# Windowed attention and mixer: first tiles with per-head maxima, weights converted behind x, inner layer two tiles behind, keys loaded first

## The chip, the core and the metric

The kernel runs on one core of a Trainium2 chip. Five engines work side by side, each through its own queue in order: TensorE (PE), VectorE (DVE), ScalarE (ACT), GpSimd (POOL) and SyncE (SP), which here issues nearly all DMAs. They wait for one another by semaphores. Matrix products land in PSUM banks; everything else lies in SBUF. The metric is the device time of one execution in microseconds (us).

## The reference

Attention over a causal window of 64 positions, and a mixer (two small MLPs, one over tokens, one over channels) on its result:

```python
scores = scale * np.matmul(q, k.transpose(0, 1, 3, 2))     # q, k, v: 8 x 8 heads x 576 x 64
mask = (rel >= 0) & (rel < 64)
scores = np.where(mask, scores, -1000000000.0)
scores = scores - np.max(scores, axis=-1, keepdims=True)
attn = np.exp(scores)
attn = attn / (np.sum(attn, axis=-1, keepdims=True) + 1e-09)
x = np.matmul(attn, v)                                     # heads side by side: 8 x 576 x 512
h = np.maximum(xt @ w_tok1, 0.0) @ w_tok2                  # xt: x transposed; inner width 256
u = x + h.transpose(0, 2, 1)
h2 = np.maximum(u @ w_ch1, 0.0) @ w_ch2                    # inner width 1536
return u + h2
```

The weights arrive as 64-bit floats.

## The kernel before

The first third of the run is one loop over 36 attention tiles (lines 499 to 561). A tile is 128 queries, two blocks of 64, of all eight heads, with the two blocks of keys that the window reaches. Heads are handled in two halves (u = 0 and 1) of four. For a tile:

- qk (scores, s): TensorE, two PSUM banks.
- softmax: the maxima, on VectorE. For the tiles up to 6, TensorE has added the mask by a matmul (line 287), so VectorE takes one reduction over four heads (line 309) and scales the result (line 310). For later tiles one operation per head adds the mask, scales, writes to SBUF and gives the maximum (line 316).
- softmax_exp: eight exponentials on ScalarE with their sums (line 325).
- pt_transpose: TensorE transposes (pp), ScalarE copies to SBUF (pt, line 334).
- av: TensorE, the weighted sum of v (xp, line 344); recip and norm on VectorE (lines 352, 353, 358) give x.
- split_x: x as a high part (xhi, ScalarE) and the rest (xlo, GpSimd), since the mixer's products are done in two parts.
- tok1: the inner layer over tokens (h, line 389), six to ten matmuls a tile, collected over the tiles of a batch. Its result goes through hhi (ScalarE, line 400) and hlo (VectorE, line 409).
- tok2: pieces of the second token layer (up, lines 430 and 437), eight for each batch, which ScalarE copies out (line 442). They fill TensorE from tile 7 on.

Between these stand the conversions of the weights, 28 jobs. Each loads a slice (raw, line 236), VectorE makes 32-bit floats of it in six operations (front part lines 204 to 207, back part lines 216 to 219), GpSimd adds (w, line 221), ScalarE writes the high part and GpSimd or, for the second token weight, VectorE the low part (t1hi, t1lo, t2hi, t2lo, line 104).

The order is written by hand: the body of the loop is the order on each engine, and JOBS, PIECES, TOK1_FROM and TOK1_SLOW say at which step a conversion, a piece of tok2 or the inner layer of a tile comes. In step i the maxima and exponentials of tile i + 1, the weighted sum of tile i and the scores of tile i + 2 are issued. After the loop the channel layers follow (three plain chunks, then pairs of chunks by a scheme with seven products), nearly all TensorE.

Of the kernel before, what the change touches and what calls it, by code (L numbers as in the profile page):

```python
# [42 lines left out]
JOBS = {i: 1 if 0 <= i < 6 or i == 12 or i > 6 and i % TPP not in (0, 3, 5) else 0 for i in range(-1, 37)}  # L43
PIECES = {22: (1, 0), 23: (1, 0), 31: (1, 0), 32: (1, 0), 33: (1, 0), 34: (1, 0), 35: (3, 0), 36: (2, 1)}

TOK1_FROM, TOK1_SLOW, TOK2_FROM = 2, 4, 7

N_PE, N_EARLY = 7, 4
# [35 lines left out]
def mixer_kernel(ctx: ExitStack, tc: tile.TileContext, qh, kh, vh, wt1, wt2, wc1, wc2, out):  # L84
# [38 lines left out]
    with ExitStack() as actx:  # L123
# [26 lines left out]
        maskr = [pa.tile([P, P], F32R, name=f"maskr{m}") for m in range(2)]  # L150
        identr = pa.tile([P, P], F32R, name="identr")
# [6 lines left out]
        def warm(k):  # L158
            for _ in range(k):
                nc.tensor.matmul(idle, zero[:, :P], zero, start=True, stop=True)  # L160

        make_identity(nc, ident)
        nc.scalar.copy(identr, ident)
        for m in (1, 0):
            nc.gpsimd.memset(mask[m], 0.0)
            for half in range(2):
                mh = mask[m][half * BLK:(half + 1) * BLK]
                nc.gpsimd.affine_select(out=mh, in_=mh, compare_op=ALU.is_ge, fill=NEG,
                                        base=-1, pattern=[[1, P]], channel_multiplier=-1)
                nc.gpsimd.affine_select(out=mh, in_=mh, compare_op=ALU.is_ge, fill=NEG,  # L170
                                        base=BLK, pattern=[[-1, P]], channel_multiplier=1)
            if m == 1:
                nc.gpsimd.memset(mask[1][0:BLK, 0:BLK], NEG)
            nc.scalar.copy(maskr[m], mask[m])
# [94 lines left out]
        def qk(i):  # L269

            qt, on_pe = loaded[i][0], i < N_PE
            s = []
            for u in range(2):

                if i == 1:
                    tag, bufs = "h", 2
                elif (i, u) == (N_PE, 1) or 2 <= i < N_PE and (2 * i + u) % 3 == 0:
                    tag, bufs = "up", 1
                else:
                    tag, bufs = "s", 2  # L280
                s.append(ps.tile([P, 4, P], F32, name=f"s{i}_{u}", tag=tag, bufs=bufs))
                s_ps[i, u] = s[u]
                if i == 0 and u == 0:
                    warm(4)
                if on_pe:
                    mk = maskr[1 if tile_blocks(i)[0][1] == 0 else 0]
                    nc.tensor.matmul(s[u], identr, mk.unsqueeze(1).to_broadcast([P, 4, P]), start=True, stop=False,
                                     skip_group_check=True)
            if i == 0:
                warm(3)  # L290
            for j in range(4):
                for u in range(2):
                    r = slice(u * BLK, (u + 1) * BLK)
                    for half, (b, n) in enumerate(tile_blocks(i)):
                        so = s[u][half * BLK:(half + 1) * BLK, j].rearrange("p (n c) -> p n c", n=2)
                        nc.tensor.matmul(so, qt[r, j, half], kbs[b][r, n:n + 2, j],  # L296
                                         start=not on_pe, stop=True, skip_group_check=on_pe)

        def softmax(i, u):
# [7 lines left out]
            nmu = nm.rearrange("p (j u) -> p j u", u=2)[:, :, u]  # L307
            if i < N_PE:
                nc.vector.tensor_reduce(out=nmu, in_=s_ps[i, u], axis=AX.X, op=ALU.max, negate=True)
                nc.vector.tensor_scalar_mul(nmu, nmu, scale)  # L310
                return
# [7 lines left out]
        def softmax_exp(i, u):  # L319
            e = e_sb[i, u]  # L320
            nm, sm = st[i]
            src, by = (s_ps.pop((i, u)), scale) if i < N_PE else (e, -1.0)
            for h in range(4):
                g = 2 * h + u
                nc.scalar.activation(e[:, h], src[:, h], AF.Exp, bias=nm[:, g:g + 1], scale=by,  # L325
                                     accum_out=sm[:, g:g + 1])
# [152 lines left out]
        job_load()  # L479
# [6 lines left out]
        load_v(0)  # L486
        nc.sync.dma_start(kbs[0][:, 8:], kh[0, :, 8:])
# [9 lines left out]
        job_convert_a()  # L497
        job_convert_b()
        qk(0)
        for i in range(-1, NT + 1):  # L500
# [13 lines left out]
            early = i < N_EARLY  # L514
# [6 lines left out]
            if i == 0:  # L521
                softmax(1, 1)
            if early and i > 0:
                norm(*normed.pop())
            if 0 <= i < NT:
                ri = recip(i)
            if i not in (4, 5):
# [10 lines left out]
            if i >= N_PE - 1:  # L538
# [4 lines left out]
            if i + 1 < NT and i != 0:  # L543
                softmax(i + 1, 1)
            if i < N_PE - 1:
                for _ in range(n_jobs):
                    job_convert_a()
            if i < N_PE - 1:
# [5 lines left out]
            if N_PE - 1 <= i < NT - 1:  # L554
                softmax_exp(i + 1, 1)
            for _ in range(n_jobs):
                job_convert_b()
            if 0 <= i < NT:
                xp = av(i, pts)
                if i + 1 < N_EARLY:  # L560
                    normed = [(i, xp, ri)]
                else:
                    norm(i, xp, ri)
            finish_h_low()
            if i + 2 < NT:
# [411 lines left out]
```

## Time and profile before

| | us |
|---|---|
| median of 3 runs | 832.0 (831.72 to 832.02) |
| the profiled execution | 832.27 |
| its span, first to last instruction | 830.5 |
| TensorE busy in the span | 814.5 (98%) |
| VectorE busy | 508.6 (61%) |
| ScalarE busy | 336.4 (41%) |
| GpSimd busy | 104.8 (13%) |

Busy time is the time in which an engine has an instruction in work. The shares are means over the whole run: VectorE and ScalarE do most of their work in the first 250 us. Most of the 16 us in which TensorE has nothing in work lie in the first 60 us. The time outside the span, 1.77 us, is start and end of the execution.

### The profile page before, as it was taken

Reading aid. Unit: us, or ns where it says so; the run is one execution under the profiler, and the core shown is the slowest. Engines: PE = TensorE matmul, PEld = TensorE weight load, DVE = VectorE, ACT = ScalarE, POOL = GpSimd, SP = SyncE. Lnnn points to the kernel's source line nnn. Section 1 sums busy time; section 2 is a strip of 40 time slices with the busy share of each in tenths; the row PEclk is TensorE's granted clock in tenths of the full one; section 3 lists DMA queues with packets and bytes.
Section 4 is the critical chain, followed back from the end, with each engine's and each line's share of the span. In section 5 each row is a group of like instructions: output and inputs, shape, how many; then the busy total and the mean of one; then the engine's idle time right before and its main releaser. Section 6 shows DMA issues by size and latency. Waiting matters only on the chain.

```text
span 830.5 us, 15190 instructions
## 1 busy us (share of the span) xinstructions
PE 814.5 (98%) x5878; PEld 678.9 (82%) x5878; DVE 508.6 (61%) x1288; ACT 336.4 (41%) x1017; POOL 104.8 (13%) x110
## 2 busy tenths in 40 slices
PE   8879999999999999999999999999999999999998
PEld 6668888888888878888888888878888888888886
DVE  6888988788782993774444535267625277525252
ACT  6788888888874440331221202033202033202020
POOL 4434543444330000000000000000000000000000
PEclk9999999999999999999999999999999999999999
DMA  9667778587545528633505442324543334532002
GB/s 346 202 216 243 237 251 277 192 280 273 179 133 196 168 82 257 203 98 120 197 1 210 157 190 95 133 95 169 168 176 117 111 120 169 175 144 89 1 1 101
DMA packets 69671, 136.51 MB, mean 164 GB/s; under 512 B 7008, under 2 KB 39264, under 8 KB 67680
## 3 DMA queue, kind: packets, MB, share of 16 engines
q1 hardware_dynamic: 67488, 133.71, 47.4%
q10 hardware_dynamic: 2112, 1.84, 0.7%
q8 instruction: 46, 0.75, 0.4%
q14 instruction: 25, 0.20, 0.1%
HBM read 104.66 MB, written 30.87 MB: 163 GB/s over the span
## 4 chain that ended last, share of the span: by engine, by line
PE 83%; DVE 9%; ACT 4%; issue 2%; DMA 1%; POOLq 0%; POOL 0%; DVEq 0%; ACTq 0%; SPq 0%
PE gp L876 19%; PE op L664 11%; PE gp L656 8%; PE up L437 5%; PE h L389 5%; PE op_2a L664 4%; PE op_4a L664 4%; PE op_0a L664 4%; PE op_0b L664 4%; PE op_2b L664 4%; PE op_4b L664 4%; PE xp L344 3%; PE s L296 3%; PE pp L332 3%; PE up L430 2%; ACT e L325 2%
## 5 line engine op out<-in xcount | busy, mean ns | idle before, releaser
L876 PE MATMUL gp<-m,w1hi 128*128 128x512 f32 x504 | 155.5, 390 | 0.7 <-DVE x L884 0.7
L876 PEld LDWEIGHTS gp<-m,w1hi 128*128 128x128 f32 x504 | 94.5, 188 | 21.0 <-DVE x L884 1.5
L876 PE MATMUL gp<-m,w1lo 128*128 128x512 f32 x252 | 98.2, 390 | 0.0
L325 ACT ACTIVATE e<-e,nm 128x128 f32<-128x128 f32 x232 | 90.7, 401 | 0.1
L643 ACT ACTIVATE ghi<-x 128x512 fp32r<-128x512 f32 x54 | 34.1, 632 | 119.9 <-DVE x L886 68.3
L880 ACT COPY x<-gp 128x512 f32<-128x512 f32 x18 | 10.4, 578 | 143.2 <-PE gp L876 143.2
L644 DVE SCALAR_TENSOR_TENSOR glo<-x,ghi 128x512 fp32r<-128x512 f32 x54 | 37.4, 693 | 38.1 <-ACT ghi L643 38.1
L643 ACT ACTIVATE ghi<-gp 128x512 fp32r<-128x512 f32 x50 | 29.8, 597 | 70.0 <-PE gp L656 70.0
L656 PE MATMUL gp<-uhi,w1hi 128*128 128x512 f32 x144 | 56.1, 390 | 0.0
L656 PE MATMUL gp<-ulo,w1hi 128*128 128x512 f32 x144 | 56.1, 390 | 0.0
L656 PE MATMUL gp<-uhi,w1lo 128*128 128x512 f32 x144 | 56.1, 389 | 0.0
L316 DVE CUSTOM_DVE_ANT_0 e<-s,mask 128x128 f32<-128x128 f32 x232 | 53.0, 285 | 4.1 <-PE s L296 3.7
L876 PEld LDWEIGHTS gp<-m,w1lo 128*128 128x128 f32 x252 | 47.3, 188 | 9.8
L664 PE MATMUL op<-ghi,w2lo 128*128 128x512 f32 x128 | 49.9, 390 | 0.0
L664 PE MATMUL op<-ghi,w2hi 128*128 128x512 f32 x128 | 49.9, 390 | 0.0
L664 PE MATMUL op<-glo,w2hi 128*128 128x512 f32 x128 | 49.9, 389 | 0.0
L644 DVE SCALAR_TENSOR_TENSOR glo<-gp,ghi 128x512 fp32r<-128x512 f32 x50 | 34.4, 688 | 25.1 <-ACT ghi L643 25.0
L344 PEld LDWEIGHTS xp<-v,pt 128*64 128x64 f32 x1152 | 36.7, 138 | 13.8 <-ACT e L325 10.2
L104 POOL TENSOR_TENSOR xlo<-x,xhi 128x512 fp32r<-128x512 f32 x32 | 41.6, 1299 | 41.4 <-ACT xhi L101 41.0
L325 ACT ACTIVATION_READ_ACCUMULATOR e<-e,nm 128x1 f32 x232 | 45.9, 198 | 0.0
L437 PE MATMUL up<-t2hi,hhi 128*128 128x320 f32 (+1 forms) x128 | 43.0, 336 | 0.0
L344 PE MATMUL xp<-v,pt 128*64 128x64 f32 x1152 | 41.5, 225 | 1.0 <-ACT pt L334 0.6
(168 smaller groups left out, 1872.2 us busy)
## 6 DMA issues: line engine op xcount, KB each, us to landing
v<-vh SPq DMA_DIRECT2D x36, 512.0 KB, 3.9
w1hi<-w1s SPq DMA_DIRECT2D x18, 896.0 KB, 4.6
w1lo<-w1s SPq DMA_DIRECT2D x18, 896.0 KB, 6.4
raw<-wc SPq DMA_DIRECT2D x32, 384.0 KB, 4.4
q<-qh SPq DMA_DIRECT2D x36, 256.0 KB, 4.8
k<-kh SPq DMA_DIRECT2D x7, 1280.0 KB, 7.4
out<-uf SPq DMA_DIRECT2D x35, 256.0 KB, 2.7
uf<-u_dram SPq DMA_DIRECT2D x8, 1024.0 KB, 9.0
```

The source lines that it names most:

```text
L104: eng_lo.tensor_sub(lo, src, hi.bitcast(F32))
L296: nc.tensor.matmul(so, qt[r, j, half], kbs[b][r, n:n + 2, j], start=not on_pe, stop=True, skip_group_check=on_pe)
L316: nc.vector.tensor_tensor_reduce(out=e[:, h], in0=s[:, h], in1=mk, scale=-scale, scalar=MAX_F32, op0=ALU.add, op1=ALU.min, accum_out=nm[:, ...
L325: nc.scalar.activation(e[:, h], src[:, h], AF.Exp, bias=nm[:, g:g + 1], scale=by, accum_out=sm[:, g:g + 1])
L344: nc.tensor.matmul(xp[half * BLK:(half + 1) * BLK, h], pts[h % 2][:, h // 2, half * BLK:(half + 1) * BLK], vt[:, half, h], start=True, sto ...
L389: nc.tensor.matmul(h_ps[b][tt], w[:, o + tt * P:o + (tt + 1) * P], x, start=first and n == 0, stop=last and n == len(combos) - 1)
L437: nc.tensor.matmul(up[:, :n], hx[:, cs], w[:, tt * S + s0:tt * S + s0 + n], start=False, stop=(k == 6), skip_group_check=True)
L643: nc.scalar.activation(hi, src, AF.Relu)
L644: nc.vector.scalar_tensor_tensor(out=lo, in0=src, scalar=0.0, in1=hi.bitcast(F32), op0=ALU.max, op1=ALU.subtract)
L656: nc.tensor.matmul(gp, w[:, w1_at(ft, ct)], x[:, ct], start=(k == 0), stop=(k == 3 * NCT - 1))
L664: nc.tensor.matmul(op, w[:, ct, ft], x[:, cols], start=(first and k == 0), stop=(last and k == 3 * len(gs) - 1), skip_group_check=not (fir ...
L876: nc.tensor.matmul(b, w[:, at], c[:, h, t], start=(n < 4 and k == 0), stop=(k == 5), skip_group_check=True)
```

## The change

Up to tile 7 the loop's steps are written in another way.

- The maxima of the first tiles are taken by the per-head operation of the later tiles (line 316); mask matmuls, and the copies of mask and identity that they used, are gone, and all exponentials read the SBUF tile.
- The first raw load goes behind the first loads of q, k and v; its conversion, which stood ahead of the loop, goes into step 0. In steps 0 to 5 a conversion stands whole behind the normalization of x. Seven conversions then stand in steps 0 to 6, where there was one ahead of the loop and six in steps 0 to 5.
- The inner layer runs two tiles behind until step 7, which takes two tiles; before, step 4 took two.
- The pieces of step 7 come both at the end; before, one stood ahead of the inner layer.
- Normalization is no longer put off by a step in the first four tiles, and five warm-up matmuls in a row stand where there were four and three.

```diff
-JOBS = {i: 1 if 0 <= i < 6 or i == 12 or i > 6 and i % TPP not in (0, 3, 5) else 0 for i in range(-1, 37)}
-PIECES = {22: (1, 0), 23: (1, 0), 31: (1, 0), 32: (1, 0), 33: (1, 0), 34: (1, 0), 35: (3, 0), 36: (2, 1)}
-
-TOK1_FROM, TOK1_SLOW, TOK2_FROM = 2, 4, 7
-
-N_PE, N_EARLY = 7, 4
+JOBS = {i: 1 if 0 <= i < 7 or i == 12 or i > 6 and i % TPP not in (0, 3, 5) else 0 for i in range(-1, 37)}
+PIECES = {7: (0, 2), 22: (1, 0), 23: (1, 0), 31: (1, 0), 32: (1, 0), 33: (1, 0), 34: (1, 0), 35: (3, 0), 36: (2, 1)}
+
+TOK1_FROM, TOK1_SLOW, TOK2_FROM = 2, 7, 7
+
+N_START = 6
...
-        maskr = [pa.tile([P, P], F32R, name=f"maskr{m}") for m in range(2)]
-        identr = pa.tile([P, P], F32R, name="identr")
...
-        def warm(k):
-            for _ in range(k):
-                nc.tensor.matmul(idle, zero[:, :P], zero, start=True, stop=True)
-
         make_identity(nc, ident)
-        nc.scalar.copy(identr, ident)
...
-            nc.scalar.copy(maskr[m], mask[m])
...
-            qt, on_pe = loaded[i][0], i < N_PE
+            qt = loaded[i][0]
             s = []
             for u in range(2):
 
-                if i == 1:
-                    tag, bufs = "h", 2
-                elif (i, u) == (N_PE, 1) or 2 <= i < N_PE and (2 * i + u) % 3 == 0:
-                    tag, bufs = "up", 1
-                else:
-                    tag, bufs = "s", 2
-                s.append(ps.tile([P, 4, P], F32, name=f"s{i}_{u}", tag=tag, bufs=bufs))
+                s.append(ps.tile([P, 4, P], F32, name=f"s{i}_{u}", tag="h" if i == 1 else "s", bufs=2))
                 s_ps[i, u] = s[u]
-                if i == 0 and u == 0:
-                    warm(4)
-                if on_pe:
-                    mk = maskr[1 if tile_blocks(i)[0][1] == 0 else 0]
-                    nc.tensor.matmul(s[u], identr, mk.unsqueeze(1).to_broadcast([P, 4, P]), start=True, stop=False,
-                                     skip_group_check=True)
-            if i == 0:
-                warm(3)
             for j in range(4):
...
-                                         start=not on_pe, stop=True, skip_group_check=on_pe)
+                                         start=True, stop=True)
...
-            nmu = nm.rearrange("p (j u) -> p j u", u=2)[:, :, u]
-            if i < N_PE:
-                nc.vector.tensor_reduce(out=nmu, in_=s_ps[i, u], axis=AX.X, op=ALU.max, negate=True)
-                nc.vector.tensor_scalar_mul(nmu, nmu, scale)
-                return
 
...
-            src, by = (s_ps.pop((i, u)), scale) if i < N_PE else (e, -1.0)
             for h in range(4):
                 g = 2 * h + u
-                nc.scalar.activation(e[:, h], src[:, h], AF.Exp, bias=nm[:, g:g + 1], scale=by,
+                nc.scalar.activation(e[:, h], e[:, h], AF.Exp, bias=nm[:, g:g + 1], scale=-1.0,
...
-        job_load()
         load_k(0)
         load_q(0)
...
         load_q(1)
         nc.sync.dma_start(k0[:, :, 2:], kh0[:, :, 2:])
         load_v(0)
+        job_load()
         nc.sync.dma_start(kbs[0][:, 8:], kh[0, :, 8:])
         load_q(2)
         job_load()
@@ -494,8 +466,8 @@
             tok1_plan[i] = range(n, m)
             n = m
 
-        job_convert_a()
-        job_convert_b()
+        for _ in range(5):
+            nc.tensor.matmul(idle, zero[:, :P], zero, start=True, stop=True)
         qk(0)
...
-            early = i < N_EARLY
...
             if i + 1 < NT:
                 softmax(i + 1, 0)
-            if i == 0:
-                softmax(1, 1)
-            if early and i > 0:
-                norm(*normed.pop())
+            if i < N_START:
+                softmax(i + 1, 1)
             if 0 <= i < NT:
                 ri = recip(i)
-            if i not in (4, 5):
+            if i > N_START:
                 while to_finish:
                     job_finish()
...
-            if i >= N_PE - 1:
+            if i >= N_START:
                 for _ in range(n_jobs):
                     job_convert_a()
             if i == NT - 1:
                 pts.append(pt_transpose(i, 1))
-            if i + 1 < NT and i != 0:
+            if N_START <= i < NT - 1:
                 softmax(i + 1, 1)
-            if i < N_PE - 1:
-                for _ in range(n_jobs):
-                    job_convert_a()
-            if i < N_PE - 1:
+            if i < N_START:
                 softmax_exp(i + 1, 1)
                 while to_finish:
                     job_finish()
             for n in tok1_plan.get(i, ()):
                 tok1(n)
-            if N_PE - 1 <= i < NT - 1:
+            if N_START <= i < NT - 1:
                 softmax_exp(i + 1, 1)
-            for _ in range(n_jobs):
-                job_convert_b()
+            if i >= N_START:
+                for _ in range(n_jobs):
+                    job_convert_b()
             if 0 <= i < NT:
-                xp = av(i, pts)
-                if i + 1 < N_EARLY:
-                    normed = [(i, xp, ri)]
-                else:
-                    norm(i, xp, ri)
+                norm(i, av(i, pts), ri)
             finish_h_low()
+            if i < N_START:
+                for _ in range(n_jobs):
+                    job_convert_a()
+                    job_convert_b()
             if i + 2 < NT:
```

On VectorE, step 5 (tile 6 has its maxima, tile 5 its normalization; c, r and raw belong to a conversion, t2lo is the low part of the second token weight, x<-xp the normalization). Before:

```order
L204 TENSOR_SCALAR c_661<-raw_518 128x384
L206 TENSOR_SCALAR c_661<-c_661 128x384
L207 TENSOR_SCALAR c_661<-c_661 128x384
L104 TENSOR_TENSOR t2lo<-w_578,t2hi 128x384
L216 SCALAR_TENSOR_TENSOR c_661<-raw_518,c_661 128x384
L218 TENSOR_SCALAR r_683<-c_661 128x384
L219 SCALAR_TENSOR_TENSOR r_683<-raw_518,r_683 128x384
L358 TENSOR_TENSOR x_706<-xp_689,ri_651 128x512
```

And now:

```order
L324 SCALAR_TENSOR_TENSOR ri_744<-sum_627 128x8
L325 RECIPROCAL ri_744<-ri_744 128x8
L104 TENSOR_TENSOR t2lo<-w_687,t2hi 128x384
L330 TENSOR_TENSOR x_786<-xp_769,ri_744 128x512
L196 TENSOR_SCALAR c_788<-raw_606 128x384
L198 TENSOR_SCALAR c_788<-c_788 128x384
L199 TENSOR_SCALAR c_788<-c_788 128x384
L208 SCALAR_TENSOR_TENSOR c_788<-raw_606,c_788 128x384
```

The first low part had half a conversion ahead of it; now it has the whole of the next conversion, and the normalization, behind it.

On TensorE, the end of step 7 (s is the scores of tile 9, up a piece of tok2, pp the transposes of tile 8). Before:

```order
L296 MATMUL s_1_1026<-k_740,q_844 64x128 x2
L430 MATMUL up_0_1_1047<-ident,x_347 128x128
L430 MATMUL up_0_1_1047<-ident,x_441 128x128
L437 MATMUL up_0_1_1047<-t2hi,hhi_0_785 128x256
L437 MATMUL up_0_1_1047<-t2lo,hhi_0_785 128x256
```

And now:

```order
L409 MATMUL up_0_0_1042<-t2hi,hhi_1_869 128x256
L409 MATMUL up_0_0_1042<-t2lo,hhi_1_869 128x256
L409 MATMUL up_0_0_1042<-t2hi,hlo_1_902 128x256
L402 MATMUL up_0_1_1053<-ident,x_274 128x128
L402 MATMUL up_0_1_1053<-ident,x_370 128x128
L409 MATMUL up_0_1_1053<-t2hi,hhi_0_867 128x256
```

Where one piece followed the scores of tile 9, the batch's first two pieces now follow each other; both use the one bank named up.

On SP, the head of the queue. Before:

```order
L236 DMA raw_141<-wt 128x320
L142 DMA q_144<-qh 128x512
L483 DMA k_143<-kh 128x2x512
L142 DMA q_147<-qh 128x512
```

And now:

```order
L142 DMA q_136<-qh 128x512
L454 DMA k_135<-kh 128x2x512
L142 DMA q_139<-qh 128x512
L456 DMA k_135<-kh 128x2x512
L147 DMA v_142<-vh 128x1024
L228 DMA raw_144<-wt 128x320
```

The first raw load has gone from the first place to the sixth.

## Rows read from the trace of the kernel before

**Rows 1.** Windows: us, then each engine's busy us (instructions), PEclk, DMA, GB/s.

```profile
40.00:50.00 10.00, 7.52 (x134) 5.74 (x130) 7.37 (x16) 7.24 (x26) 3.61 (x3) 1.00 0.77 270
...
60.00:70.00 10.00, 10.00 (x168) 8.58 (x168) 9.69 (x38) 8.21 (x35) 3.65 (x4) 1.00 0.55 181
```

**Rows 2.** Chain of waits, 45 to 68 us: start us, us, what.

```profile
49.10 0.56 DVE t2lo L104
...
51.71 0.61 DVE hlo L409
...
52.46 2.76 PE h L389 x10
...
59.29 1.38 PE h L389 x6
...
63.88 0.87 PE pp L332 x8
```

**Rows 3.** Timeline, 0 to 9 us: start us, us, instruction, idle before.

```profile
1.18 3.78 PE L160 MATMUL idle<-zero 128*128 128x256 f32 x8 [1.18 <-DVE zero L155]
...
1.65 0.43 SPq L483 DMA_DIRECT2D k<-kh  x1
...
7.67 1.10 PE L296 MATMUL s<-k,q 64*64 64x128 f32 x32
...
8.80 0.69 DVE L309 TENSOR_REDUCE nm<-s 128x4 f32<-128x512 f32 x1 [2.50 <-PE s L296]
```

**Rows 4.** DMA issues at 1.6 to 2.0 us: size, us to landing.

```profile
k<-kh SPq DMA_DIRECT2D x1, 512.0 KB, 5.6
```

**Rows 5.** Timeline, VectorE, one conversion: its first and last operation.

```profile
13.06 0.28 DVE L204 TENSOR_SCALAR c<-raw 128x320 int32<-128x320 int32 x1
...
15.05 0.49 DVE L219 SCALAR_TENSOR_TENSOR r<-raw,r 128x320 f32<-128x320 uint32 x1
```

**Rows 6.** Groups, ScalarE, 0 to 57 us: busy us, mean ns; idle before.

```profile
L334 ACT COPY pt<-pp 128x512 f32<-128x512 f32 x14 | 7.6, 590 | 1.8 <-PE pp L332 1.8
L101 ACT CAST xhi<-x 128x512 fp32r<-128x512 f32 x5 | 3.1, 621 | 4.2 <-DVE x L358 4.2
L325 ACT ACTIVATE e<-e,nm 128x128 f32<-128x128 f32 x8 | 3.1, 396 | 0.0
L101 ACT CAST t1hi<-w 128x320 fp32r<-128x320 f32 x4 | 1.9, 462 | 2.5 <-POOL w L221 2.4
```

**Rows 7.** Groups, VectorE, 0 to 57 us.

```profile
L310 DVE TENSOR_SCALAR nm<-nm 128x4 f32<-128x4 f32 x14 | 4.8, 342 | 0.5
L358 DVE TENSOR_TENSOR x<-xp,ri 128x512 f32<-128x512 f32 x7 | 4.8, 683 | 1.0 <-PE xp L344 1.0
```

**Rows 8.** Timeline, 52 to 54 us: per-head maxima of tile 7 beside GpSimd.

```profile
52.44 1.29 POOL L104 TENSOR_TENSOR xlo<-x,xhi 128x512 fp32r<-128x512 f32 x1 [0.19 <-ACT xhi L101]
...
52.83 0.28 DVE L316 CUSTOM_DVE_ANT_0 e<-s,mask 128x128 f32<-128x128 f32 x1
...
53.66 0.17 DVE L352 SCALAR_TENSOR_TENSOR ri<-sum 128x8 f32<-128x8 f32 x1
```

**Rows 9.** Timeline, GpSimd and VectorE together, at 64 and 87 us.

```profile
63.97 1.28 POOL L104 TENSOR_TENSOR xlo<-x,xhi 128x512 fp32r<-128x512 f32 x1 [0.24 <-ACT xhi L101]
63.99 1.28 DVE L352 SCALAR_TENSOR_TENSOR ri<-sum 128x8 f32<-128x8 f32 x1
...
86.50 1.01 POOL L104 TENSOR_TENSOR w1lo<-w,w1hi 128x384 fp32r<-128x384 f32 x1 [1.50 <-ACT w1hi L101]
...
87.04 0.89 DVE L216 SCALAR_TENSOR_TENSOR c<-raw,c 128x384 int32<-128x384 int32 x1
```

**Rows 10.** Groups, GpSimd, 0 to 57 us.

```profile
L104 POOL TENSOR_TENSOR xlo<-x,xhi 128x512 fp32r<-128x512 f32 x5 | 6.5, 1306 | 0.5 <-ACT xhi L101 0.4
L221 POOL TENSOR_TENSOR w<-r,c 128x320 f32<-128x320 f32 x4 | 3.5, 872 | 12.5 <-DVE r L219 12.5
L104 POOL TENSOR_TENSOR t1lo<-w,t1hi 128x320 fp32r<-128x320 f32 x4 | 3.5, 868 | 3.5 <-ACT t1hi L101 3.5
```

## Prediction

> **What bounds the kernel now.** I read the windows first. From 60 us TensorE is busy in the whole slice, while at 40 to 50 us it is busy 7.52 of 10 us [rows 1]; the change lies in that unfilled part. The chain of waits came next [rows 2]. It leaves TensorE before 52.46 us and goes through VectorE: the low part of the second inner weight (t2lo, 49.10), the rest of a conversion, the low part of the inner activation (hlo, 51.71). Only then can the ten inner matmuls of 52.46 start, and from there it is TensorE without a gap to 63.88, where the loop's step of tile 7 ends (its last work is the second tok2 piece; then come the pp transposes of tile 8). So the change is worth what it does to that instant: the same work lies behind it, on an engine that is full. The profiled execution took 832.27 us (span 830.5, 1.77 around it), 0.27 above the median of 832.0. I work out how 63.88 moves and add that to the median.
>
> **The change part by part.**
>
> *Start.* The scores of tile 0 begin at 7.67, and the first maximum 1.13 later, at 8.80 [rows 3]. Their keys are issued at 1.65 [rows 3] and land 5.6 us after that [rows 4], at 7.25. The change takes a 320 KB load from in front of them. The gain is at least 0, since less lies ahead of them, and at most 1.8, since five warm-ups at 3.78/4 us from 1.18 on [rows 3] end at 5.9. I take 0.85 for the keys: half a microsecond of issue and a part of the 320 KB, so 6.4, and the scores then need not wait for a last warm-up. First maximum: 6.4 + 1.13, say 7.55. The fourteen mask matmuls and three copies of masks and identity that go lie where TensorE and ScalarE wait for VectorE: worth 0; were TensorE full there, 14 matmuls of 0.23 (a sixth of 1.38 [rows 2], same width) would be 3.2.
>
> *Conversion of weights.* One conversion is 2.5 us of VectorE (13.06 to 15.05 + 0.49) [rows 5]. Before, the first lies under the wait for the keys. Now it stands in the loop, behind the first x, on the engine that sets the pace. From the first maximum at 7.55: 0.4 to the first exponential, eight exponentials at about 0.39 (0.396 [rows 6]) 3.1, two pt copies 1.2 [rows 6], the weighted sum 0.65, the normalization 0.65 (0.683 [rows 7], the next one starts a little early), the conversion 2.5. The maxima of tile 2 then start at 16.1, with one conversion done, where before two were done. So the lead of the start is paid to the conversion. The load itself is passed by q, three k and v loads on SP's queue; it is used at 13.6, and if it took 7 us from an issue near 3.1 it is there.
>
> *Maxima.* Before, a tile costs two reductions of 0.69 [rows 3] and two scalings of 0.342 [rows 7], 2.06 us, as nothing overlaps. Now eight operations that start 0.21 apart (52.83 to 53.66 for four [rows 8]): 1.66. Seven tiles give back 2.8.
>
> *Waits for GpSimd.* The scaling is two times the 0.17 of an undisturbed one because VectorE waits while GpSimd runs. The clearest rows: the reciprocal's first operation L352 started at 63.99, just behind GpSimd's xlo (63.97, 1.28 long), and took 1.28 itself; the conversion's L216 at 87.04 ended 0.41 after GpSimd's subtraction of 86.50 [rows 9]. Per-head maxima, which read PSUM and one mask, show no such wait: four of them keep their 0.21 under an xlo that runs from 52.44 to 53.73 [rows 8]. Now put the new order on GpSimd's times [rows 10]. Let M be the start of a tile's maxima. The add of the last conversion runs M+0.16 to M+1.03, xlo to M+2.3. The reciprocal is due at M+1.66 and waits to M+2.3. Normalization starts M+2.6, conversion M+3.2, its L216 is due at M+4.25. On ScalarE the exponentials run M+0.4 to M+3.5, the high part of the weight 0.46 more [rows 6], so GpSimd subtracts t1lo from M+4.04 to M+4.91. L216 waits 0.66, ends 0.4 later, and with L218 and L219 the next tile's maxima start at M+6.27. ScalarE alone would need 1.18 + 0.62 + 3.1 + 0.46 = 5.4, so VectorE sets the pace, and exponentials that read SBUF cost nothing while it does (rival 2 prices ScalarE's pace).
> The Trainium skill (SBUF — State Buffer, Who interferes with whom) says that a VectorE instruction with two SBUF inputs, or in a two-port mode, and one of GpSimd exclude each other for the whole instruction, and that one reading a single SBUF input does not. The two waiting rows agree. By that rule L218 and L219 wait too, which no row here shows; if only what rows show waits, about 0.5 us of the sum below goes.
> Step by step: maxima of tile 2 at 16.1; of tile 3 at 22.7 (t1lo meets L218 instead); tile 4 at 28.9; tile 5 at 35.2; tile 6 at 42.0 (wider conversion, 0.2, and the two casts behind the last t1lo).
>
> *The low part t2lo.* It now stands ahead of the normalization and the conversion of tile 5 and waits for ScalarE, whose high part is behind all eight exponentials of tile 6 (42.4 to 45.5, plus 0.55). VectorE idles from 44.4: t2lo 46.1, normalization 46.6, conversion 47.2 to 49.9. Then half the maxima of tile 7 (to 50.7), reciprocal behind GpSimd's add (51.1), front of the last conversion behind xlo (53.1), other half (53.95), back part (55.4), normalization (56.0), hlo done 56.65.
>
> *Tail of the stage.* Before, TensorE ran 63.88 - 52.46 = 11.4 us behind hlo. Now tiles 6 to 8 of the attention are done by then, and left are ten inner matmuls (six take 1.38 [rows 2], so 2.3), and the stretch from 59.29 to 63.88, 4.59 us, which ends on one piece; to 63.6. The first piece of the pair must come on top. Before it stood apart; now both stand together, on one bank. The second waits until ScalarE has copied the first, and that copy is queued behind xhi of tile 7, which needs its normalization, which is behind a conversion: 63.5 + 0.62 + 0.4 (half a pt copy, bound 0 to 0.59) = 64.55, with hand-over and 1.05 for the piece 65.7.
> Sum: 65.7 - 63.88 = +1.8, with everything later unchanged: 833.8 us against the median.
>
> **The rivals.**
> 1. *GpSimd's subtraction misses the conversion.* L216 is due 0.2 us behind t1lo's start; were it first, most of that wait is gone. Tile steps then are about 5.6, four of them and the casts give back 2.9: 62.8, -1.1, 830.9. For it: a margin of 0.2 us over seven tiles. Against it: VectorE's next operation, L218, then runs into the same 0.87 us.
> 2. *The port waits don't arise and ScalarE sets the pace* (faster). Steps of 5.4: exponentials of tile 2 to 6 begin 17.3, 22.65, 28.0, 33.4, 39.3; t2lo 43.0, conversion to 46.8, hlo 52.7, pair of pieces done 61.8: -2.1, 829.9. It decides from the point at which conversions in the loop run in 2.5 us. For it: the conversion at 13.06 did [rows 5]. Against it: GpSimd was idle then.
> 3. *The keys land no earlier*, since the queues share the transfers: 0.85 later throughout, 834.7. For it: five loads are in flight; against: 320 KB fewer are ahead.
> 4. *TensorE's clock falls*, as it has only 4.4 us of work in a step of 6.27 (scores 1.1 [rows 3], inner layer 1.38 and transposes 0.87 [rows 2], the weighted sum about as long as the scores). At half the rate that is 8.8, 2.5 over the step; two such tiles cost 5, 838 with the rest of the forecast. Against it: the clock is 1.00 at 40 to 50 us with a quarter of the time idle [rows 1].
>
> **How the numbers follow.** Forecast (833.8, own range 832.4 to 835.2) 0.47; rival 1 0.23 (830.2 to 831.8); rival 2 0.14; rival 3 0.08; rival 4 0.04; 0.04 for a change that the full TensorE hides anyhow, 832. A measurement tells 0.2% from no change, 1.66 us, so faster is below 830.3, slower above 833.7. Faster: nearly all of rival 2 and a fifth of rival 1, 0.18. Slower: a little over half of the forecast, rivals 3 and 4, 0.39. Same: 0.43. The range, 829.9 to 835.4, leaves out the lower half of rival 2, rival 4 and the edges.
>
> **What would show it.** Right: scores of tile 0 near 6.4; maxima of tiles 3, 4 and 5 about 6.2 apart with L352 and L216 stretched; VectorE idle before t2lo; hlo near 56.6; the pp transposes of tile 8 near 65.7. Wrong: tile steps of 5.6 or less, hlo before 54, or TensorE waiting in the stretch past 65 us where it was full.

## The result and the profile after

The changed kernel took 833.33 us (median of 20 executions, 832.52 to 835.46) against 832.01 (831.16 to 833.73) of the kernel before on the same chip: ratio 1.0016, 95% interval 1.0009 to 1.0022, so +1.3 us where +1.8 was forecast. By the forecast's bound of 0.2% (slower from 833.7 on) that is no change, though the interval lies above 1. The profiled execution took 833.98 us (span 832.2).

The windows that answer to [rows 1], with the slice between them (us, then busy us of each engine, PEclk, DMA share, GB/s):

```profile
40.00:50.00 10.00, 5.76 (x96) 4.27 (x91) 8.58 (x38) 6.78 (x29) 5.30 (x5) 0.92 0.61 208
50.00:60.00 10.00, 7.56 (x48) 6.47 (x49) 9.09 (x37) 7.05 (x25) 2.73 (x3) 0.57 0.42 145
60.00:70.00 10.00, 9.54 (x138) 8.05 (x137) 7.46 (x32) 6.31 (x25) 4.24 (x4) 1.00 0.38 121
```

TensorE has less work at 40 to 50 us (5.76 against 7.52), VectorE more (8.58 against 7.37), and the granted clock, 1.00 in both slices of before, is 0.92 and then 0.57. The chain of waits of the changed kernel, 43 to 67 us, answers to [rows 2] (start us, us, engine, tile and line; the maxima are now L289, the inner matmuls L361, hlo L381, tok2 L402 and L409):

```profile
43.85 0.41 ACT t2hi L101
...
49.49 1.19 DVE c L196
...
52.44 1.97 PE s L274 x28
54.41 1.90 PE pp L304 x8
56.31 4.82 PE h L361 x16
...
64.37 0.38 ACT u L414
...
64.79 0.44 PE up L402 x2
...
65.95 0.87 PE pp L304 x8
```

The instant that the prediction followed, pp of tile 8, moves from 63.88 to 65.95; the span grows by 1.7. The last 28 of the 32 matmuls of the scores take 1.97 us, where all 32 took 1.10 [rows 3], and the transposes 1.90 where they took 0.87 [rows 2]. Sixteen inner matmuls take 4.82; six took 1.38 [rows 2], which makes 3.7. In all thirteen profiles that are read here, the fastest (e11, 62.19) and the slowest (e5, 74.14) among them, the execution's time is 768.0 to 768.7 us more than the start of pp of tile 8 in TensorE's timeline: the instant that the prediction followed does set the time.

The start, TensorE of the changed kernel (answers to [rows 3]: start us, us, instruction, idle before):

```profile
1.19 3.81 PE L470 MATMUL idle<-zero 128*128 128x256 f32 x10 [1.19 <-DVE zero L153]
5.12 1.10 PE L274 MATMUL s<-k,q 64*64 64x128 f32 x32
8.57 1.10 PE L274 MATMUL s<-k,q 64*64 64x128 f32 x32 [2.35 <-DMA k<-kh]
```

Tile 0 starts 2.55 us earlier than before, directly behind the five warm-up matmuls; tile 1 waits for the second part of the keys. And one conversion in the loop, all engines (answers to [rows 9]):

```profile
25.12 0.44 ACT L101 CAST t1hi<-w 128x320 fp32r<-128x320 f32 x1
...
25.62 0.49 DVE L208 SCALAR_TENSOR_TENSOR c<-raw,c 128x320 int32<-128x320 int32 x1
25.64 1.20 POOL L104 TENSOR_TENSOR t1lo<-w,t1hi 128x320 fp32r<-128x320 f32 x1 [2.06 <-ACT t1hi L101]
...
26.21 0.80 DVE L210 TENSOR_SCALAR r<-c 128x320 int32<-128x320 int32 x1
```

L208 and L210 are L216 and L218 of before. GpSimd's t1lo, issued 0.02 behind L208, takes 1.20 instead of 0.868 [rows 10]: it ends 1.22 behind L208's start, that is 0.73 behind L208's end. L210 comes while it runs, ends 0.17 behind it and takes 0.80 instead of 0.33. The stretched one of each pair is the one that began second. The Trainium skill (SBUF — State Buffer, Who interferes with whom) says that whichever of the two issues first holds the shared ports for its whole instruction, and that this includes single-input operations in a two-port mode; L210, which has one input, agrees with its 0.80. The prediction found no row for that, but the trace of the kernel before has some:

```profile
45.72 1.33 DVE L206 TENSOR_SCALAR c<-c 128x384 f32<-128x384 f32 x1
```

This one runs beside GpSimd's xlo of 45.47 (1.36 long); undisturbed, L206 takes 0.36. So these waits are not new. Added up over the timelines from the maxima of tile 2 to those of tile 6, what VectorE's operations take above their undisturbed times is about 4.2 us before the change and 3.9 after it (an estimate).

### The profile page after: what moved, and what is told of

The parts are those of the page before. It is cut to its first block, busy times and chain, and to the rows that moved or that the text cites. A ratio compares the mean times of both kernels' runs of the same rounds, so it can differ in the third digit from the quotient of the medians.

```text
span 832.2 us, 15257 instructions
## 1 busy us (share of the span) xinstructions
PE 812.4 (98%) x5860; PEld 678.7 (82%) x5860; DVE 508.7 (61%) x1372; ACT 337.5 (41%) x1014; POOL 105.9 (13%) x110
## 4 chain that ended last, share of the span: by engine, by line
PE 82%; DVE 10%; ACT 3%; issue 2%; DMA 2%; POOLq 0%; SPq 0%; POOL 0%; DVEq 0%; ACTq 0%
PE gp L843 19%; PE op L631 11%; PE gp L623 8%; PE up L409 5%; PE h L361 5%; PE op_4a L631 4%; PE op_2b L631 4%; PE op_2a L631 4%; PE op_0b L631 4%; PE op_0a L631 4%; PE op_4b L631 4%; PE s L274 3%; PE xp L316 3%; PE pp L304 3%; PE up L402 2%
## 5 line engine op out<-in xcount | busy, mean ns | idle before, releaser
L297 ACT ACTIVATE e<-e,nm 128x128 f32<-128x128 f32 x288 | 112.3, 397 | 12.4 <-DVE nm L289 12.3
L289 DVE CUSTOM_DVE_ANT_0 e<-s,mask 128x128 f32<-128x128 f32 x288 | 65.3, 284 | 11.3 <-PE s L274 11.1
L297 ACT ACTIVATION_READ_ACCUMULATOR e<-e,nm 128x1 f32 x288 | 56.0, 195 | 0.0
L274 PE MATMUL s<-k,q 64*64 64x128 f32 x1152 | 43.2, 280 | 10.4 <-DVE nm L289 4.1
L274 PEld LDWEIGHTS s<-k,q 64*64 64x64 f32 x1152 | 33.4, 135 | 14.5 <-issue 10.6
```

The lines of the kernel that those rows point to most:

```text
L289: nc.vector.tensor_tensor_reduce(out=e[:, h], in0=s[:, h], in1=mk, scale=-scale, scalar=MAX_F32, op0=ALU.add, op1=ALU.min, accum_out=nm[:, ...
L297: nc.scalar.activation(e[:, h], e[:, h], AF.Exp, bias=nm[:, g:g + 1], scale=-1.0, accum_out=sm[:, g:g + 1])
```

## The experiments

Each was timed in five rounds beside the kernel before, whose median on those chips was 831.7 to 831.8; all start from the changed kernel but e6. Ratios are to the kernel before.

**e1_fill.** Two groups of matmuls of zeros in an unused bank, where TensorE idles:

```diff
+            if i == 8:
+                idle2 = ps.tile([P, 256], F32, name="idle2", tag="up", bufs=1)
+                for _ in range(4): nc.tensor.matmul(idle2, zero[:, :P], zero, ...)
             for u in range(2): ...          # the two score tiles
+                    if i == 8 and (j, u) == (0, 1):
+                        for _ in range(5): nc.tensor.matmul(idle2, ...)
```

> The changed kernel with nine matmuls of zeros on TensorE, four ahead of the scores of tile 8 and five between their two halves, where TensorE idled 2.33 and 2.72 us. Theory (the clock at half rate from about 49 to 58.5 us costs time): granted clock 1.00 through 45 to 60 us, the scores' second half and the pp transposes take about 1.0 us each and not 1.97, and the inner matmuls come 0.23 apart; then the scores of tile 9 wait for VectorE's maxima of tile 8, which end near 60.3, and the pp transposes of tile 8 start near 64.0 and not 65.9: 1.5 to 2 us faster than the changed kernel, about 831.5. Rival (VectorE's chain sets the stage, the slow matmuls lie beside it): clock 1.00 but pp still near 65.9 and 833.3.

Measured: 832.42 us, ratio 1.0007 (0.9998 to 1.0016). Windows from 45 us on, first of the kernel before, then of the changed one, then of this one:

```profile
45.00:50.00 5.00, 4.33 (x76) 3.40 (x76) 3.24 (x7) 4.97 (x21) 1.75 (x2) 1.00 0.85 315
50.00:52.50 2.50, 0.04 (x1) 0.07 (x1) 2.43 (x6) 0.80 (x3) 1.05 (x2) 1.00 0.60 236
```

```profile
45.00:50.00 5.00, 2.08 (x38) 1.36 (x36) 4.79 (x18) 2.45 (x11) 1.77 (x2) 0.84 0.24 51
50.00:52.50 2.50, 0.06 (x4) 0.09 (x5) 2.43 (x12) 1.75 (x7) 0.45 (x1) 0.50 1.00 390
52.50:56.00 3.50, 3.50 (x37) 3.17 (x37) 3.36 (x11) 2.03 (x8) 1.84 (x2) 0.50 0.37 88
56.00:60.00 4.00, 4.00 (x14) 3.22 (x13) 3.30 (x18) 3.27 (x13) 0.43 (x1) 0.67 0.11 43
```

```profile
45.00:50.00 5.00, 4.28 (x49) 3.07 (x48) 4.79 (x19) 2.45 (x9) 1.30 (x2) 1.00 0.27 83
50.00:52.50 2.50, 2.29 (x10) 1.69 (x10) 2.43 (x10) 1.74 (x7) 0.92 (x1) 1.00 0.95 360
```

Before the change TensorE had nothing in 50 to 52.5 us either (0.04), but 4.33 us of work in the 5 us ahead of it, and stayed at 2.4 GHz. In the changed kernel there are 2.08, and it fell to 1.2 GHz (0.50). With the zeros it stays at 1.00 up to 60 us, and the chain of this run starts the inner matmuls from hlo:

```profile
54.90 0.61 DVE hlo L388
...
55.65 3.96 PE h L368 x16
...
64.42 0.88 PE pp L311 x8
```

From the start of the maxima of tile 6 (40.75 here, 40.29 in the changed kernel) to pp of tile 8 it is 23.67 us against 25.66: 2.0 gained in this pair of profiles. The median gained only 0.75 (1.0016 to 1.0007), less than expected, and the intervals overlap; e12 comes back to this.

**e2_t2lo.** In the step of tile 5 the split of t2 stands behind the normalization:

```diff
-                while to_finish:
+                while to_finish and i < N_START - 1:
                     job_finish()
...
                 norm(i, av(i, pts), ri)
+            while to_finish and i == N_START - 1:
+                job_finish()
```

> The changed kernel with the split of the second inner weight that stood ahead of the normalization of tile 5 put behind it, so that VectorE need not wait 1.18 us for t2hi. Theory (that wait is on the path): the normalization of tile 5 at 43.1, first half of the maxima of tile 7 at about 46.8 instead of 48.0, and all behind it 1.2 earlier: 832.1 if TensorE's clock still falls, about 830.5 if the shorter idle time keeps it at 1.00. Rival (VectorE is not what the stage waits for): pp of tile 8 stays near 65.9, 833.3.

Measured: 832.97 us, ratio 1.0011 (1.0002 to 1.0020). That lies between the two forecasts, and the interval holds the changed kernel's 1.0016, so no gain is shown. VectorE's timeline:

```profile
46.04 0.56 DVE L104 TENSOR_TENSOR t2lo<-w,t2hi 128x384 fp32r<-128x384 f32 x1 [0.38 <-ACT t2hi L101]
```

Only the normalization (44.97 to 45.66) slipped under the wait; t2lo still waits for t2hi, which is behind eight exponentials. From the maxima of tile 2 to those of tile 7 it is 32.44 us (16.72 to 49.16) instead of 32.86 (15.14 to 48.00), and the clock fell all the same. VectorE's chain got 0.4 us shorter; moving one instruction across the wait does not remove it.

**e3_keys.** The first weight load goes in front of the keys again:

```diff
+        job_load()
         load_k(0)
...
         load_v(0)
-        job_load()
```

> The changed kernel with the first raw weight load in front of the keys again, as before the change. Theory (the start carries through, since VectorE is full from 9.8 to 42 us): scores of tiles 0 and 1 about 1.2 us later (6.3 and 9.8), maxima of tiles 2 to 6 1.2 later, pp of tile 8 near 67.1, about 834.5. Rival (the 1.67 us that VectorE idles between the maxima of tiles 0 and 1, and the idle time before t2lo, take it up): maxima of tile 6 at 40.3 as now, 833.3.

Measured: 835.31 us (five executions), ratio 1.0037 (1.0025 to 1.0050), 1.75 us over the changed kernel. TensorE's start:

```profile
6.95 1.49 PE L274 MATMUL s<-k,q 64*64 64x128 f32 x32 [1.91 <-DMA k<-kh]
8.86 1.98 PE L274 MATMUL s<-k,q 64*64 64x128 f32 x32 [0.42 <-DMA k<-kh]
```

Tile 0 is 1.83 later and the maxima of tile 2 come at 16.86, 1.72 later, those of tile 6 at 42.00, 1.71 later. The start carries through unabridged. Part of the 1.72 is TensorE at half rate here (1.98 for the scores of tile 1, not 1.10).

**e4_nosub.** t1lo is set to zero once; GpSimd's subtraction for it is left out:

```diff
+        nc.gpsimd.memset(t1lo.bitcast(F32), 0.0)
...
-                    split(nc.scalar, eng, hi[:, o:o + m], lo[:, o:o + m], w)
+                    if src is wt1: nc.scalar.copy(hi[:, o:o + m], w)
+                    else: split(nc.scalar, eng, hi[:, o:o + m], lo[:, o:o + m], w)
```

> The changed kernel without GpSimd's subtraction for t1lo (t1lo is set to zero once at the start, so the low part of the first inner weight is left out of the result). Theory (VectorE's conversion waits while that subtraction runs): the operations L208 and L210, stretched to 0.80 to 1.12 us in tiles 2 to 5, fall to 0.33 to 0.56, steps of a tile from 6.2 to 5.7 us, maxima of tile 6 near 38.3 instead of 40.3, pp of tile 8 near 64 and 831.3. Rival (another wait of the same length takes its place, ScalarE or the next operation on GpSimd): steps stay near 6.2 and the time at 833.3.

Measured: 831.21 us, ratio 0.9994 (0.9985 to 1.0003), 1.8 us under the changed kernel. Groups of VectorE, 0 to 57 us (mean ns of one before the bar's end), first of the changed kernel, then here, where the lines are one higher:

```profile
L210 DVE TENSOR_SCALAR r<-c 128x320 int32<-128x320 int32 x4 | 2.3, 564 | 0.3
L208 DVE SCALAR_TENSOR_TENSOR c<-raw,c 128x384 int32<-128x384 int32 x3 | 2.2, 744 | 0.1
```

```profile
L209 DVE SCALAR_TENSOR_TENSOR c<-raw,c 128x384 int32<-128x384 int32 x3 | 1.7, 558 | 0.1
L211 DVE TENSOR_SCALAR r<-c 128x320 int32<-128x320 int32 x4 | 1.3, 326 | 0.3
```

The maxima of tiles 2 to 6 start at 15.07, 20.75, 26.43, 32.18, 38.19: steps of 5.68 to 6.01 instead of 6.16 to 6.58. About 0.5 us a tile is VectorE's wait for t1lo, as expected, and no other wait took its place.

**e5_inner.** The inner layer one tile behind again from tile 4 on: `TOK1_SLOW` 4 and not 7.

> The changed kernel with the inner layer one tile behind from tile 4 on, as before the change (maxima, conversions, loads and t2lo stay changed). In the changed kernel TensorE has 0.69 us of work between idle times of 2.33 and 2.72 us, in the kernel before 4.2 us of work between 2.27 and 2.67, and only there the clock stays at 1.00. Theory (the lag of two tiles piles sixteen inner matmuls behind the idle time and leaves nothing between its halves): with the lag undone the granted clock stays at 1.00 from 45 to 60 us, pp of tile 8 starts 1.5 to 2 us earlier, near 64, about 831.5. Rival (the maxima, not the lag, starve TensorE of scores): the clock falls all the same, and the time stays near 833.1.

Measured: 841.67 us, ratio 1.0116 (1.0102 to 1.0130), so both forecasts failed on the time. The clock fell as well (0.56 at 40 to 45 us, 0.79 at 45 to 50), so the theory failed on that too. TensorE's timeline at its two longest waits after 45 us:

```profile
48.02 0.80 PE L361 MATMUL h<-xhi,t1hi 128*128 128x512 f32 x1 [2.80 <-POOL xhi L342]
...
58.72 0.79 PE L361 MATMUL h<-xlo,t1hi 128*128 128x512 f32 x1 [3.77 <-POOL xlo L104]
```

TensorE takes its work in order, and these matmuls stand ahead of the weighted sum. One tile behind, they wait for splits on GpSimd that stand behind the conversion's add; the normalization waits for the weighted sum, the next conversion for the normalization. With the conversions where they now stand, the loop needs the lag of two tiles; undoing it makes the idle time longer, so the lag is not its cause.

**e6_max_alone.** The kernel before with the per-head maxima alone:

```diff
-            qt, on_pe = loaded[i][0], i < N_PE
+            qt, on_pe = loaded[i][0], False
...
-            if i < N_PE:                    # tensor_reduce and scaling
+            if False:
...
-            src, by = (s_ps.pop((i, u)), scale) if i < N_PE else (e, -1.0)
+            src, by = e, -1.0
```

> The kernel before with one part of the change alone: the maxima of tiles 0 to 6 by the per-head operation with the mask added on VectorE, so no mask matmuls; the emission order, the conversions, the loads and the inner layer as before. Theory of the prediction (VectorE sets the pace of the first tiles, 2.06 against 1.66 us a tile): 0.4 us a tile, 2.8 over seven tiles, the pp transposes of tile 8 at about 61.1 instead of 63.88, about 829. Rival (the 0.34 us of the scaling was a wait for GpSimd, which only moves to the next operation, and ScalarE or TensorE's idle time takes up the rest): less than 1 us, 831 to 832.

Measured: 831.62 us, ratio 0.9998 (0.9989 to 1.0007). The first maxima of tiles 2 and 6 in VectorE's timeline:

```profile
14.66 0.29 DVE L316 CUSTOM_DVE_ANT_0 e<-s,mask 128x128 f32<-128x128 f32 x1
...
41.93 0.28 DVE L316 CUSTOM_DVE_ANT_0 e<-s,mask 128x128 f32<-128x128 f32 x1
```

In the kernel before they start at 16.18 and 43.27. So 1.52 us are gained by tile 2, where TensorE also has the scores earlier (13.53 and not 15.04), and nothing after it: from tile 2 to tile 6 it is 27.27 us, and 27.09 before. The 0.4 us a tile of the theory do not appear, as the rival said. The inner matmuls behind hlo start at 51.41 and not 52.46 [rows 2]. Then its windows:

```profile
50.00:52.50 2.50, 1.09 (x3) 0.94 (x4) 2.50 (x11) 1.80 (x4) 2.11 (x2) 0.70 0.05 20
52.50:56.00 3.50, 3.50 (x33) 2.68 (x33) 1.75 (x13) 3.28 (x17) 0.18 (x1) 0.73 0.00 0
```

The clock falls here too, and pp of tile 8 starts at 63.84, where it was (63.72 in the same view of before). In this profile the clock takes back the 1.05 us that were left at hlo. Its mean clock, 0.995, is at the low end of the run's executions (0.995 to 0.998), so for the median that is not shown.

**e7_swap and e8_swap_fill.** The casts and subtractions of a weight go between the two halves of the exponentials; e8 has the zeros of e1 as well:

```diff
             if i < N_START:
-                softmax_exp(i + 1, 1)
                 while to_finish:
                     job_finish()
+                softmax_exp(i + 1, 1)
```

> The changed kernel with one line moved: in the first six steps the casts and subtractions of a converted weight are emitted ahead of the second half of the exponentials, not behind it. GpSimd's t1lo then runs from about 2.4 to 3.4 us behind the start of a tile's maxima, beside the normalization, and t2hi comes 1.6 us earlier. Theory (L208 and L210 wait because t1lo falls into the conversion; t2lo waits because t2hi is behind all eight exponentials): steps of a tile 5.7 to 5.8 instead of 6.16, maxima of tile 6 at about 38.6, first half of the maxima of tile 7 near 45.0 instead of 48.0, pp of tile 8 near 62.8 with TensorE's clock falling as it does now, about 830.2. Rival (t1lo then collides with the front of the conversion, or the exponentials, later by the cast, become the bound): steps near 6.2 and 832 to 833.

> The kernel of the run before with the nine matmuls of zeros around the scores of tile 8 as well. If the two causes are separate their gains add: granted clock 1.00 up to 60 us, pp of tile 8 near 61.5, about 829.3. If the filling only hides a wait that the moved casts remove anyway, it stays at the time of the run before.

Measured: 832.41 us, ratio 1.0006 (0.9998 to 1.0015), and 830.68 us, ratio 0.9984 (0.9976 to 0.9993). In e7, all engines:

```profile
18.71 0.86 POOL L104 TENSOR_TENSOR t1lo<-w,t1hi 128x320 fp32r<-128x320 f32 x1 [0.54 <-ACT t1hi L101]
...
19.14 0.61 DVE L196 TENSOR_SCALAR c<-raw 128x320 int32<-128x320 int32 x1
...
20.51 0.49 DVE L208 SCALAR_TENSOR_TENSOR c<-raw,c 128x320 int32<-128x320 int32 x1
...
21.11 0.33 DVE L210 TENSOR_SCALAR r<-c 128x320 int32<-128x320 int32 x1
```

L208 and L210 are free and the first conversion operation pays instead (0.61, not 0.32), so the steps are 5.99, 5.97, 5.68 and 6.08: the rival holds in part. VectorE no longer waits for t2hi, but the subtraction for t2lo now runs beside one of GpSimd's and takes 1.59 us and not 0.56, which gives back most of the 1.18:

```profile
42.37 1.59 DVE L104 TENSOR_TENSOR t2lo<-w,t2hi 128x384 fp32r<-128x384 f32 x1
```

The maxima of tile 7 come 31.23 us behind those of tile 2 (32.86 before the move). The clock still fell, and the gain of the median, 0.8 us, is less than half of the 2.9 expected. Filling the idle time then gains another 1.8 us, with intervals apart: it does not only hide a wait that the moved casts remove.

**e9_start_fill.** Three more matmuls of zeros behind the first scores:

```diff
         qk(0)
+        for _ in range(3): nc.tensor.matmul(idle, zero[:, :P], zero, ...)
```

> The changed kernel with three matmuls of zeros behind the scores of tile 0, where TensorE waits 2.35 us for the second part of the keys. In one profile of this start (the run with t2lo moved) the clock was 0.93 and 0.90 in the first two slices of 10 us, the scores of tile 1 took 1.99 us and the maxima of tile 2 came at 16.7 instead of 15.1. Theory (in a part of the executions the clock falls here too, and it makes the spread of the times): the granted clock is 1.00 from 0 to 20 us, the slowest times (834 to 835.5) go, the median falls by 0.3 to 0.6 us, near 832.7. Rival (the start varies by when the keys land): same median, same spread; by as much as 1.3 us slower where keys land early.

Measured: 833.57 us, ratio 1.0020 (1.0011 to 1.0029), that of the changed kernel on the same chip. The spread stayed (832.5 to 834.3). The rival's forecast holds: filling this gap alone is worth nothing that can be measured. One execution of the eleven took 4583 us; it is left out of the spread, and as it is the profiled one, no profile of this run is read.

**e10_pieces.** `PIECES` without its entry for tile 7, so one tok2 piece in each slot.

> The changed kernel with the tok2 pieces of tile 7 one in each slot of the step, as before the change, and not both in the second. Theory of the prediction (the pair on one bank costs a copy and a hand-over): the 0.46 us that TensorE waits for the copy goes, pp of tile 8 at about 65.4, 832.6. Rival (a piece in the first slot needs t2lo, which VectorE has done only near 58.4 us, and stands on TensorE ahead of the sixteen inner matmuls that start at 56.3): these start near 59.5, by then at full clock or not, and pp of tile 8 comes 1 to 3 us later, 834 to 836.

Measured: 834.24 us, ratio 1.0028 (1.0018 to 1.0039). TensorE in the first slot:

```profile
57.54 0.38 PE L409 MATMUL up<-t2hi,hhi 128*128 128x256 f32 x1 [0.88 <-ACT t2hi L101]
58.19 0.39 PE L409 MATMUL up<-t2lo,hhi 128*128 128x256 f32 x1 [0.27 <-DVE t2lo L104]
...
58.53 0.39 PE L361 MATMUL h<-xlo,t1hi 128*128 128x512 f32 x1
```

The piece waits for the last part of t2 and holds the inner matmuls to 58.53, as the rival said, but pp of tile 8 comes at 65.39, 25.38 us behind the maxima of tile 6 (40.01), where e12 has 24.58 (64.95 in the same view): 0.8 later, less than the rival expected; by then the clock is back (0.39 for an inner matmul). The median is 0.6 us over that of e12, with overlapping intervals. So the pair in the second slot is not the worse order, though it costs 0.46 for the copy.

**e11_best and e12_changed_again.** e8 and e9 together, and the changed kernel unaltered, on one chip.

> The changed kernel with the casts of a converted weight ahead of the second half of the exponentials, the nine matmuls of zeros around the scores of tile 8, and three behind the scores of tile 0. Theory (three separate causes): granted clock 1.00 to 60 us, pp of tile 8 near 62.5, about 830.3, in all executions. Rival (the start's three matmuls hold up the scores of tile 1): 831 to 831.5.

> The changed kernel again, beside the other three on one chip, to compare them directly: 833.0 to 833.3, pp of tile 8 at 65.8 to 66.5, and the granted clock below 1.00 between 45 and 60 us again if that belongs to the kernel and not to one execution.

Measured: 830.30 us, ratio 0.9986 (0.9977 to 0.9995), against 833.65, ratio 1.0020 (1.0011 to 1.0029): 3.3 us apart. Windows of e11:

```profile
40.00:50.00 10.00, 9.27 (x98) 7.01 (x98) 9.69 (x34) 7.11 (x28) 4.90 (x5) 1.00 0.71 257
50.00:60.00 10.00, 8.76 (x122) 6.88 (x121) 9.69 (x42) 7.27 (x29) 2.72 (x3) 1.00 0.25 82
```

e11 beats the kernel before by 1.2 us (0.4 to 1.9) and is as fast as e8; its pp of tile 8 starts at 62.19. Windows and chain of e12:

```profile
50.00:52.50 2.50, 0.00 (x0) 0.00 (x1) 2.43 (x12) 1.74 (x7) 0.54 (x1) 0.50 0.98 391
52.50:56.00 3.50, 3.47 (x36) 3.17 (x37) 3.36 (x9) 2.03 (x8) 1.76 (x2) 0.50 0.33 89
56.00:60.00 4.00, 4.00 (x18) 3.23 (x16) 3.29 (x18) 3.28 (x13) 0.51 (x1) 0.90 0.10 37
```

```profile
56.40 3.90 PE h L361 x16
...
65.11 0.87 PE pp L304 x8
```

The clock falls again, but is back sooner (0.90 at 56 to 60 and not 0.67): the inner matmuls take 3.90, not 4.82, and pp of tile 8 comes at 65.11, 24.74 us behind the maxima of tile 6 (40.37), where e1 took 23.67. The mean clock over the span is 0.996 in all eleven executions here and in 17 of the 20 of the first comparison, 0.993 in the one profiled there. By these pairs of profiles the fall costs 1.1 us in an execution with the usual mean clock and 2.0 in the first profile, which would explain why e1 gained less at the median. The size stays open, though: over e7, with a mean clock of 0.995 or 0.996 in ten of its eleven executions, the zeros of e8 gained 1.8 us at the median.

## Why the prediction was right, and where not

The forecast held: 833.8 was 0.5 us too high, and "no change" was its likeliest class (0.43, with 0.39 for slower; 833.8 itself lies just past its bound of 833.7). But the mechanism is half the forecast one: VectorE came earlier than forecast and TensorE's clock fell, and the two errors nearly cancel. That they do is luck.

- **What bounds.** Right: pp of tile 8 moved by 2.07 in the profile and the span by 1.7; in the other eleven profiles too the time follows that instant.
- **Start.** Too late by about 1 us. The scores of tile 0 came at 5.12 and not 6.4, a gain of 2.55 where the text has "at most 1.8": the five warm-up matmuls end at 5.00 and not 5.9. In the kernel before TensorE had no idle time ahead of these scores [rows 3], so the warm-ups and masks in front of them held them as well as the keys; with the old load order (e3) and the new warm-ups they come at 6.95. The step also overlooked that tile 1 waits for the second part of the keys (8.57), which gave back a part: maxima of tile 2 at 15.14, forecast 16.1. At the median the load order is worth 1.75 us (e3).
- **Conversion in the loop.** Right: 12.77 to 15.22 on VectorE, 2.45 us.
- **Maxima.** The 0.4 us a tile are not there (e6). The price of 2.06 counted the wait for GpSimd in the scalings as their own time; undisturbed, the two reductions and scalings of tile 0 take 1.70 us in the kernel before (8.80 to 10.50), the eight per-head operations 1.69 (6.37 to 8.06). The sum goes by 1.66 for the new ones and does not depend on it.
- **Waits for GpSimd.** Right, and shown: steps of 6.16, 6.16, 6.25 and 6.58 (forecast 6.6, 6.2, 6.3 and 6.8). The wait for t1lo took 0.5 us a tile (e4). It fell on L208 in two tiles and on L210 in the other two. Rivals 1 and 2, steps of 5.6 and 5.4, did not come about.
- **t2lo.** Right in kind, 1.18 us of idle time (1.7 forecast), and two us early with all ahead of it: t2lo at 44.29 (46.1), first half of the maxima of tile 7 at 48.00 (49.9).
- **hlo.** The step to 56.65 counts one of its two subtractions, and that is what counts: in e1 the pair runs from 54.82 to 56.10, and the first inner matmul starts at 55.65, while the second subtraction still runs. In the changed kernel that first one is done near 55.0 (54.34 and 0.68), 1.65 earlier than forecast.
- **Tail.** Forecast 9.05 us behind hlo. At full clock (e1) it is 8.9, from the end of hlo's first subtraction, 55.51, to 64.42. The copy between the pieces did not wait behind xhi of tile 7; the hand-over of 0.46 is all that the pair cost.
- **The step that was wrong: the tail was priced at full clock, and rival 4, TensorE's clock, had a chance of 0.04.** It was argued against with the clock of 1.00 at 40 to 50 us of before, a quarter of it idle. But the forecast itself ended the two halves of the maxima of tile 7 more than 3 us apart (50.7 and 53.95), and the scores of tile 8 wait for both: 4 of their 32 matmuls, 0.69 us of work, stand between idle times of 2.33 and 2.72. The clock fell there, and it did so in every profile of the changed kernel and its variants without the zeros there (e2, e3, e4, e5, e7, e10, e12). Priced at 5 us (which with the forecast is 838.8 and not 838), it cost 1.1 to 2.0, since only the scores, the transposes and some of the inner matmuls ran at the low rate.

Worked forward from the forecast of 65.7: hlo earlier by 1.65, the tail shorter by 0.15, the clock 1.1 to 2.0 longer, gives 65.0 to 65.9; measured were 65.11 (e12) and 65.95. Since the price of the clock is itself taken from these profiles, this checks the first two terms only. Rival 3 (keys no earlier) is refuted by the row at 5.12.

That e6 lost its gain to the clock is read from the windows of one profile and was not tried with filled idle time. Why the scores of tile 0 start up to 0.6 us apart from one execution to another (5.12 to 5.75 in the profiles of this load order) stays open. VectorE does 203 of its 509 busy us in the first 250 us, not most of them as the section on time and profile has it.

## What to carry to other kernels

Where a faster engine lets another one idle in two long pieces with little between, look at the granted clock of the stretch behind: the work there can take twice its time, and a few matmuls of zeros in an unused bank can win it back (e8, 1.8 us). An operation's mean time in a trace can hold a wait for GpSimd: price a cheaper replacement against the undisturbed time, since here the wait only moved to another operation. Moving the cast that triggers GpSimd's work moves the wait as well, and takes a part of it away (e7). Where weights come later in the order, their consumers may have to come later too: undoing the lag alone cost 8 us (e5).

## What the runs showed that I had not expected

GpSimd's instruction is stretched as well as VectorE's: t1lo took 1.02 to 1.20 us in all four tiles, 0.868 before [rows 10] and 0.86 in e7. And the mean of TensorE's granted clock is 0.993 to 0.996 in the 31 executions of the changed kernel and 0.997 to 1.0 in all but one (0.996) of the 84 of the kernel before that were timed beside the experiments, though its busy time in 40 to 50 us is only 1.8 us less than before.
